# Start of a fused attention and feed-forward kernel: order of the w_in quarters, and of the first group's matmuls around the second chunk's numerators

## The chip, the cores and the metric

The kernel runs on one core of one Trainium2 chip. The core has a matrix engine (TensorE, PE in the profile), a vector engine (VectorE, DVE), an activation engine (ScalarE, ACT), a general engine (GpSimd, POOL) and SyncE (SP), which issues most DMA transfers. Each engine runs its own list of instructions in the written order and waits on semaphores for the others. The metric is the device time of one execution in microseconds; lower is better.

## The reference, cut to what matters

```python
# q, k, v: [4 batches, 4 heads, 1088 tokens, 32]; S1, S2: [8, 32]; w_in: [128, 2048]; w_out: [2048, 128]
def phi(x):                                # 64 features of a head's token
    a = einsum('rd,bhsd->bhsr', S1, x)
    b = einsum('rd,bhsd->bhsr', S2, x)
    return einsum('bhsi,bhsj->bhsij', a, b).reshape(..., 64)
q_p, k_p = phi(q), phi(k)
kv  = einsum('bhsf,bhsd->bhfd', k_p, v)    # sums over all tokens of a batch
z   = sum(k_p, axis=2)
num = einsum('bhsf,bhfd->bhsd', q_p, kv)
den = einsum('bhsf,bhf->bhs', q_p, z)[..., None] + 1e-06
x   = (num / den), heads side by side      # [4352 tokens, 128]
h   = x @ w_in
g   = h - tanh(h)
out = g @ w_out
```

All inputs and the output are 32-bit floats. The kernel uses `g @ w_out = x @ (w_in @ w_out) - tanh(h) @ w_out`, with bf16 operands in the feed-forward part.

## The kernel before

**Work.** A batch's 1088 tokens are 34 blocks of 32. The queries are handled in five chunks: chunk 0 is the first 12 blocks of batch 0, chunk 1 the other 22, and chunks 2 to 4 are batches 1 to 3. The feed-forward part runs over ten groups of tokens, of 12, 10, 12, 16, 16, 16, 16, 16, 14 and 8 blocks. Group 0 (384 tokens) is just chunk 0, group 1 (320 tokens) comes from chunk 1.

**Steps of a batch's keys** (names as in the lists of order). `kp` (PE, L553) projects the transposed keys `kT` (DVE, L542); `kab` (DVE, L559) transposes the result; `gram` (PE, L584), `gm` (DVE, L590) and `fold` (PE, L593) make the weights for the denominators; `wk` (DVE and POOL, L573) forms the key products; `sum` (PE, L609) adds them up against v. Then `kvz` (ACT, L619) copies the sums out of PSUM, `turn` (PE, L629) transposes them, and `ndw` (ACT, L636) copies the transposed sums to SBUF, as the weights of the numerators.

**Steps of a query chunk.** `qp` (PE, L679 for chunk 0, L700 for the others) projects, `qab` takes the result out of PSUM (ACT L691 for chunk 0, DVE L706), `au`, `dn`, `rd`, `an` make the denominators, `qm` (DVE and POOL, L724) the products, `qt` (DVE, L731) transposes them into `qpT`, `num` (PE, L746) multiplies them with `ndw` into PSUM banks 0 to 3, and `x` (L769; ACT for chunks 0 and 1) casts the result into the bf16 tile `xT`.

**Steps of a group.** There are 16 slices of 128 hidden units. For slice k, `h` (PE, L838) is the first layer, `t` (ACT, L841) the tanh of it, `o` (PE, L889) the second layer, added up in one bank. Slices are numbered through: group 0 has h0 to h15, group 1 h16 to h31, group 2 h32 and on. The h's rotate over three PSUM banks, so that h of slice k+3 has to wait until t of slice k has read its bank; o of slice k waits for t of slice k. For groups 7 to 9 the slices go in pairs (L829, L832), and the last group has a form of its own (L854).

**The weights.** w_in comes in four quarters of 512 columns (`wi0` to `wi3`, SP, L495), each cast to bf16 by `wic0` to `wic3` (L775, three on ACT and one on POOL). Slices 0 to 3 of each group need quarter 0, slices 4 to 7 quarter 1, and so on. Once all four are cast, SP issues a DMA transpose of w_in (`wT`, L782); from it PE computes w_in @ w_out (`wp`, L787), and DVE splits that product in two bf16 parts, `whi` and `wlo`. w_out comes in three pieces, cast by POOL (L778).

**The order.** Nothing is scheduled when the program is built. A table holds the list of steps of each engine, word for word; a second list (sessions) says in which order the users of each PSUM bank come; a third (gates) adds waits that only pace the loads and POOL's work (`k2.0<o9`: the load k2.0 waits for o9). Semaphore waits are worked out from the data, the banks and the gates. In PE's list, entries such as `$2` and `!1` are matmuls on constants whose result nobody reads.

Of the kernel before, what the change touches and what calls it, by code (L numbers as in the profile page):

```python
# [40 lines left out]
class Program:  # L41
# [203 lines left out]
DB = 7  # L245
QB = (1, 1)
QBASE = {1: 4}
WIC = ('scalar', 'gpsimd', 'scalar', 'scalar')
KCUTS = ((('vector', 0, 8), ('gpsimd', 22, 29), ('vector', 8, 16), ('gpsimd', 29, 36), ('vector', 16, 22)), (('gpsimd', 12, 24), ('vector', 0, 12), ('vector', 24, 30), ('gpsimd', 30, 36)), (('gpsimd', 12, 24), ('vector', 0, 12), ('vector', 24, 30), ('gpsimd', 30, 36)), (('gpsimd', 12, 24), ('vector', 0, 12), ('vector', 24, 30), ('gpsimd', 30, 36)))
SCUTS = (((0, 4), (4, 9)), ((0, 9),), ((0, 9),), ((0, 9),))  # L250
QCUTS = ((('vector', 0, 2), ('gpsimd', 2, 4)), (('gpsimd', 2, 4), ('vector', 0, 2)), (('gpsimd', 0, 2), ('gpsimd', 2, 4)), (('gpsimd', 0, 2), ('gpsimd', 2, 4)), (('gpsimd', 0, 2), ('gpsimd', 2, 4)))
# [20 lines left out]
ORDERS = {  # L272
    "tensor": """
~52 sk ~17 kp0 sk2 *4 ^1 gram0 qp0 fold0 *2 ^1 qpu0 sum0.0 sum0.4 qp1 turn0 $2 num0.0 num0.1 !1 h0 h1 h2 o0 h3 o1 h4
o2 h5 o3 h6 h7 kp1 h8 o4 h9 o5 h10 gram1 o6 h11 o7 fold1 h12 o8 h13 o9 num1.0 num1.1 h14 o10 h15 o11 o12 h30 h22 h20
wp h19 h18 h32 h31 o13 o14 h47 o15 h24 lin0.whi h16 lin0.wlo h17 qp2 h42 h23 lin1.whi h25 lin1.wlo o16 o17 h21 o18 o19
h29 o20 h28 h27 o21 o22 o23 h26 o24 o25 h34 h39 o26 o27 h38 o28 h43 kp2 h33 o29 o30 h35 o31 h46 h45 gram2 lin2.whi h40
fold2 lin2.wlo sum1.0 h36 h44 o32 o33 o34 turn1 o35 h37 h41 o36 num2.0 num2.1 o37 o38 o39 o40 o41 o42 h51 h49 o43 o44
# [25 lines left out]
x4.2 out6 out7 out8 out9.0  # L304
""",
    "gpsimd": """
id0 id1 au1.0 kTz0 qTz0 vz1 identb au1.1 kTz1 wqz vz0 wk0.22 wk0.29 qm0.2 qTz1 wic1 woc0 qm1.2 woc1 woc2 wk1.30 wk1.12
au2 an2 qm2.2 qm2.0 wk2.30 au3 wk2.12 an3 qm3.2 qm3.0 wk3.12 au4 wk3.30 an4 qm4.0 qm4.2
""",
    "sync": """  # L310
s2 k0.0 q0.1 q0.0 q0.2 v0.1 v0.0 v0.2 v0.3 wi0 wi3 wi2 wi1 wo0 k1.0 wo1 wo2 wT q1.0 k2.0 v1.0 q3.0 v1.1 st0.0.3
st0.0.1 v1.2 v1.3 v2.2 q2.0 st0.0.0 st0.0.2 v2.1 st2.0.2 st1.0.3 v3.1 v2.0 v2.3 v3.0 v3.3 st2.0.0 st1.0.1 st1.0.0
st2.0.1 st2.0.3 st1.0.2 k3.0 st3.0.0 st4.0.3 v3.2 st3.0.1 st3.0.2 st3.0.3 st4.0.0 st5.2.3 st5.0.3 st4.0.2 st4.0.1
st6.0.0 st6.0.2 st5.2.0 st5.0.2 st5.0.1 st5.2.1 st6.0.3 st5.0.0 st5.2.2 st7.0.0 st7.0.2 st7.0.3 st7.4.0 st7.4.2
# [24 lines left out]
def bass_polysketch_attn__then__act_tanh_shrink_kernel(nc, q, k, v, S1, S2, moe_w_in, moe_w_out, out):  # L339
# [20 lines left out]
    def act(n):  # L360
        return 75 + n / 1.2
# [411 lines left out]
    def casts():  # L773
        for x, eng in enumerate(WIC):
            P.op(f"wic{x}", eng, act(512) if eng == "scalar" else 620, lambda e, x=x, eng=eng: (e.copy if eng == "scalar" else e.tensor_copy)(  # L775
                w_in[:, 512 * x:512 * x + 512], w_in_f[:, 512 * x:512 * x + 512]), r=[("w_in_f", x)], w=[("w_in", x)])
# [216 lines left out]
```

## Time and profile before

| quantity | us |
|---|---|
| three runs | 104.47, 104.50, 105.26 |
| median of the runs | 104.5 |
| the profiled execution | 105.19 |
| its span, first to last instruction | 103.4 |
| PE busy | 94.6 (91%) |
| ACT busy | 78.6 (76%) |
| DVE busy | 54.4 (53%) |
| POOL busy | 34.8 (34%) |

The rows below and in the prediction are of the profiled execution, in microseconds from its first instruction; some 1.8 us of its time lie outside the span. The busy share of PE is high because matmuls are pipelined and overlap; what matters is where an engine stands still and for whom. The granted clock of PE was full in the whole span (the row of 40 slices):

```profile
PEclk9999999999999999999999999999999999999999
```

A row of the timeline has the start, the busy time, the engine, the line, the operation, the tiles written and read, the count of instructions that were merged, and in brackets the idle time just before with the engine that ended it. A row of the chain of waits has the start, the duration and the piece of work.

### The profile page before, as it was taken

The numbers are of one execution on the slowest core, as the hardware profiler recorded it, in microseconds if no ns is written. First come the engines' busy times: TensorE is split into PE (matmuls) and PEld (weight loads), VectorE is DVE, ScalarE is ACT, GpSimd is POOL, SyncE is SP. The second block draws the span as 40 slices with busy tenths as digits, with TensorE's granted clock in tenths as the row PEclk, the third lists the DMA queues.
The fourth block names the chain that finished last, engine by engine and source line by source line (L and its number), as shares of the span: only waits on it lengthen the run. The fifth ranks groups of instructions, "written<-read, shape, count | busy, mean of one in ns | idle before, by whom it ended". The sixth has DMA issues, their size and how long they took to land.

```text
span 103.4 us, 3175 instructions
## 1 busy us (share of the span) xinstructions
PE 94.6 (91%) x1358; PEld 49.3 (48%) x1370; DVE 54.4 (53%) x95; ACT 78.6 (76%) x156; POOL 34.8 (34%) x42
## 2 busy tenths in 40 slices
PE   7999778997999999999998999999999999999950
PEld 6647442455454665433544435345544434546740
DVE  2579997850975968884166936550756020020210
ACT  3212459858989862899996989889878999999930
POOL 2156469400655980028960000559910000000000
PEclk9999999999999999999999999999999999999999
DMA  2999999935078147037446100081031005404234
GB/s 70 360 243 271 368 319 172 301 85 202 6 222 205 40 141 182 0 63 193 86 74 205 37 6 0 1 150 27 10 53 23 6 0 79 73 6 76 39 60 95
DMA packets 25967, 11.76 MB, mean 114 GB/s; under 512 B 19808, under 2 KB 24416, under 8 KB 25952
## 3 DMA queue, kind: packets, MB, share of 16 engines
q1 hardware_dynamic: 25624, 11.15, 44.8%
q10 hardware_dynamic: 328, 0.40, 1.3%
q8 instruction: 11, 0.18, 0.7%
q14 instruction: 4, 0.03, 0.1%
HBM read 8.79 MB, written 2.23 MB: 107 GB/s over the span
## 4 chain that ended last, share of the span: by engine, by line
PE 70%; POOL 7%; DMA 6%; SPq 4%; ACT 3%; DVE 3%; issue 2%; POOLq 0%
PE ps L889 23%; PE ps L838 17%; PE ps L829 8%; PE ps L746 7%; DMA w_in_f<-in_moe_w_in_dram 6%; POOL qp L724 4%; PE ps L881 3%; PE ps L700 2%; PE ps L609 2%; PE ps L854 2%; PE ps L553 2%; ACT tt L841 2%; SPq L489 2%; POOL wk L573 1%; DVE qab L706 1%
## 5 line engine op out<-in xcount | busy, mean ns | idle before, releaser
L841 ACT ACTIVATE tt<-ps 128x512 bf16<-128x512 f32 (+2 forms) x112 | 52.7, 552 | 9.3 <-PE ps L838 5.0
L889 PE MATMUL ps<-tt,w_out 128*128 128x512 bf16 (+3 forms) x141 | 39.2, 355 | 0.5 <-ACT tt L841 0.3
L838 PE MATMUL ps<-xT,w_in 128*128 128x512 bf16 (+2 forms) x107 | 33.0, 353 | 2.4 <-ACT xT L769 1.3
L889 PEld LDWEIGHTS ps<-tt,w_out 128*128 128x128 bf16 x144 | 13.9, 98 | 12.6 <-issue 1.1
L832 ACT ACTIVATE tt<-ps 128x1024 bf16<-128x1024 f32 (+2 forms) x24 | 18.4, 859 | 0.5
L838 PEld LDWEIGHTS ps<-xT,w_in 128*128 128x128 bf16 x112 | 10.0, 98 | 17.4 <-ACT tt L841 10.8
L724 POOL TENSOR_TENSOR qp<-an,qab 128x1152 f32<-128x1152 f32 (+2 forms) x8 | 15.4, 1925 | 2.9 <-DVE an L717 2.4
L731 DVE STREAM_TRANSPOSE qpT<-qp 128x1152 f32<-128x1152 f32 (+2 forms) x10 | 11.2, 1126 | 8.7 <-POOL qp L724 8.7
L573 POOL TENSOR_TENSOR wk<-kab 128x384 f32<-128x384 f32 (+2 forms) x8 | 9.0, 1126 | 20.0 <-PE ps L889 19.5
L894 DVE STREAM_TRANSPOSE osb<-ps 128x512 f32<-128x512 f32 (+3 forms) x9 | 5.9, 657 | 17.4 <-PE ps L889 17.0
L829 PE MATMUL ps<-xT,w_in 128*128 128x512 bf16 (+2 forms) x48 | 12.1, 335 | 0.1
L746 PE MATMUL ps<-qpT,ndw 32*32 32x288 f32 (+4 forms) x320 | 6.9, 352 | 0.4 <-DVE qpT L731 0.3
L829 PEld LDWEIGHTS ps<-xT,w_in 128*128 128x128 bf16 x48 | 4.5, 98 | 4.6 <-ACT tt L832 1.2
L542 DVE STREAM_TRANSPOSE kT<-kraw 128x512 f32<-128x512 f32 (+1 forms) x8 | 5.6, 720 | 1.0 <-DMA kraw<-in_k_dram 1.0
L706 DVE STREAM_TRANSPOSE qab<-ps 128x1152 f32<-128x1152 f32 (+1 forms) x4 | 5.1, 1273 | 1.4 <-PE ps L700 1.4
L769 DVE CAST xT<-ps 128x576 bf16<-128x576 f32 (+2 forms) x7 | 4.4, 686 | 2.7 <-PE ps L746 2.7
L711 POOL TENSOR_TENSOR au<-qab 128x288 f32<-128x288 f32 x3 | 2.4, 791 | 10.0 <-DVE qab L706 7.0
L656 DVE STREAM_TRANSPOSE qT<-qraw 128x1088 f32<-128x1088 f32 (+2 forms) x5 | 5.3, 1065 | 0.7 <-DMA qraw<-in_q_dram 0.7
L746 PEld LDWEIGHTS ps<-qpT,ndw 32*32 32x32 f32 x320 | 4.0, 103 | 3.2 <-DVE qpT L731 2.0
L559 DVE STREAM_TRANSPOSE kab<-ps 128x576 f32<-128x576 f32 x4 | 3.1, 773 | 3.6 <-PE ps L553 3.6
L424 PE MATMUL ps<-const-bfloat16-1.0 128*32 128x256 bf16 x69 | 4.2, 417 | 0.8 <-PEq L978 0.8
L609 PE MATMUL ps<-wk,vx 128*32 128x64 f32 x288 | 4.8, 220 | 0.0
(82 smaller groups left out, 78.8 us busy)
## 6 DMA issues: line engine op xcount, KB each, us to landing
kraw<-in_k_dram SPq DMA_DIRECT2D x3, 544.0 KB, 4.9
qraw<-in_q_dram SPq DMA_DIRECT2D x3, 544.0 KB, 3.8
vx<-in_v_dram SPq DMA_DIRECT2D x8, 144.0 KB, 3.0
vx<-in_v_dram SPq DMA_DIRECT2D x8, 128.0 KB, 3.2
w_in_f<-in_moe_w_in_dram SPq DMA_DIRECT2D x4, 256.0 KB, 6.1
out_dram<-osb SPq DMA_DIRECT2D x12, 64.0 KB, 2.0
out_dram<-osb SPq DMA_DIRECT2D x12, 48.0 KB, 2.2
w_out_f<-in_moe_w_out_dram SPq DMA_DIRECT2D x2, 256.0 KB, 7.5
```

Source lines behind the costliest of these rows:

```text
L573: P.op(f"wk{b}.{n0}", eng, (dve if eng == "vector" else pool)(64 * n), lambda e, n0=n0, n1=n1, n=n, a_=a_: e.tensor_tensor(out=wk[0][:, n0 ...
L609: ins = e.matmul(ps[32 * h:32 * h + 32, SB, 0:64], vx[i][:, h, t, :], wk[0][:, 4 * t + h, :], start=(t == 0), stop=(t == 8), tile_position ...
L706: P.op(f"qab{u}", "vector", dve(32 * n), lambda e: e.transpose(out=qab[ui][:, 0:n, :].rearrange("p (h t) x -> p h t x", h=H), in_=ps[:, b0 ...
L724: P.op(f"qm{u}.{h0}", eng, (pool if eng == "gpsimd" else dve)(64 * (n1 - n0)), lambda e, n0=n0, n1=n1, b_=b_: e.tensor_tensor(out=qp[ui][: ...
L731: P.op(f"qt{u}.{h0}", "vector", dve(64 * (n1 - n0)), lambda e, n0=n0, n1=n1: e.transpose(out=qpT[ui][:, n0:n1, :, :].rearrange("p n y j -> ...
L746: ins = e.matmul(ps[32 * h:32 * h + 32, ct, 0:32 * own[ct]], ndw[i][32 * ct:32 * ct + 32, y, 32 * h:32 * h + 32], qpT[ui][32 * ct:32 * ct ...
L829: P.op(f"h{s + y}", "tensor", pe(n), lambda e, jb=jb, b0=b0, y=y: e.matmul(ps[:, b0 + y, 0:n], w_in[:, 128 * (jb + y):128 * (jb + y) + 128 ...
L832: P.op(f"t{s}", "scalar", act(2 * n), lambda e, ts=ts, b0=b0: e.activation(out=tt[:, ts:ts + 2, 0:n], in_=ps[:, b0:b0 + 2, 0:n], func=AF.T ...
L838: P.op(f"h{s}", "tensor", pe(n), lambda e, jb=jb, bk=bk: e.matmul(ps[:, bk, 0:n], w_in[:, 128 * jb:128 * jb + 128], xT[:, t0:t0 + n], star ...
L841: P.op(f"t{s}", "scalar", act(n), lambda e, ts=ts, bk=bk: e.activation(out=tt[:, ts, 0:n], in_=ps[:, bk, 0:n], func=AF.Tanh, scale=-1.0), ...
L889: P.op(f"o{slot + jb}", "tensor", pe(n), lambda e, jb=jb, ts=ts: e.matmul(acc[:, 0:n], w_out[:, jb, :], tt[:, ts, 0:n], start=late and jb ...
L894: P.op(f"out{g}", "vector", dve(n), lambda e: e.transpose(out=osb[u][:, 0:n], in_=acc[:, 0:n]), r=ka, w=[("osb", u)], prio=when)
```

## The change

Four things are moved; no instruction is added or removed.

- The quarters of w_in are loaded in the order 0, 1, 2, 3 (before: 0, 3, 2, 1).
- The quarter that POOL casts is the last of w_in (before: quarter 1). It keeps its place in POOL's list, and it is the transfer issued fourth in both kernels.
- On ACT, the sums' copies `kvz0` and `ndw0` stand right behind the first cast; the other two casts follow them.
- On PE, in group 0, `kp1` moves from behind h7 to behind o3, ahead of h6. h6 to h9 then follow without o's between, `gram1` has one o less ahead of it, `fold1` one o less and one h (h12) more, and `num1` (the numerators of chunk 1) goes from between o9 and h14 to behind h15. The list of bank users follows.

```diff
-WIC = ('scalar', 'gpsimd', 'scalar', 'scalar')
+WIC = ('scalar', 'scalar', 'scalar', 'gpsimd')
...
     "tensor": """
...
-o2 h5 o3 h6 h7 kp1 h8 o4 h9 o5 h10 gram1 o6 h11 o7 fold1 h12 o8 h13 o9 num1.0 num1.1 h14 o10 h15 o11 o12 h30 h22 h20
+o2 h5 o3 kp1 h6 h7 h8 h9 o4 h10 gram1 o5 h11 o6 h12 fold1 o7 h13 o8 h14 o9 h15 num1.0 num1.1 o10 o11 o12 h30 h22 h20
...
     "scalar": """
-k0.1 s1 act0 kap0 wq0u qab0 wic0 wic3 kvz0 ndw0 wic2 x0.0 t0 t1 t2 t3 t4 t5 t6 t7 t8 t9 t10 t11 t12 t13 t14 t15 x1.0
+k0.1 s1 act0 kap0 wq0u qab0 wic0 kvz0 ndw0 wic1 wic2 x0.0 t0 t1 t2 t3 t4 t5 t6 t7 t8 t9 t10 t11 t12 t13 t14 t15 x1.0
...
     "gpsimd": """
-id0 id1 au1.0 kTz0 qTz0 vz1 identb au1.1 kTz1 wqz vz0 wk0.22 wk0.29 qm0.2 qTz1 wic1 woc0 qm1.2 woc1 woc2 wk1.30 wk1.12
+id0 id1 au1.0 kTz0 qTz0 vz1 identb au1.1 kTz1 wqz vz0 wk0.22 wk0.29 qm0.2 qTz1 wic3 woc0 qm1.2 woc1 woc2 wk1.30 wk1.12
...
     "sync": """
-s2 k0.0 q0.1 q0.0 q0.2 v0.1 v0.0 v0.2 v0.3 wi0 wi3 wi2 wi1 wo0 k1.0 wo1 wo2 wT q1.0 k2.0 v1.0 q3.0 v1.1 st0.0.3
+s2 k0.0 q0.1 q0.0 q0.2 v0.1 v0.0 v0.2 v0.3 wi0 wi1 wi2 wi3 wo0 k1.0 wo1 wo2 wT q1.0 k2.0 v1.0 q3.0 v1.1 st0.0.3
```

The instructions of ACT at the start, before. The cast behind `d_wi0` is that of the first quarter; `d_wi3` is the semaphore of the quarter that is loaded second:

```order
L691 COPY qab<-ps 128x12x16
L775 CAST w_in<-w_in_f 128x512 [waits d_wi0]
L775 CAST w_in<-w_in_f 128x512 [waits d_wi3]
L619 COPY kvz<-ps 128x256 [waits s_tensor]
L636 COPY ndw<-ps 128x256 [waits s_tensor]
L775 CAST w_in<-w_in_f 128x512 [waits d_wi2]
L769 CAST xT<-ps 128x384 [waits s_tensor]
```

The same place of ACT's list after:

```order
L691 COPY qab<-ps 128x12x16
L775 CAST w_in<-w_in_f 128x512 [waits d_wi0]
L619 COPY kvz<-ps 128x256 [waits s_tensor]
L636 COPY ndw<-ps 128x256 [waits s_tensor]
L775 CAST w_in<-w_in_f 128x512 [waits d_wi1]
L775 CAST w_in<-w_in_f 128x512 [waits d_wi2]
L769 CAST xT<-ps 128x384 [waits s_tensor]
```

The copy of the sums and the copy of their transpose no longer stand behind a cast that waits for the second transfer; two casts now stand between them and the cast of chunk 0's numerators.

PE in group 0, before, from o2 (the first row) to gram1; each L838 row is one h or more, each L889 row an o, L553 is kp1 and L584 gram1:

```order
L889 MATMUL ps<-tt,w_out 128x384
L838 MATMUL ps<-xT,w_in 128x384
L889 MATMUL ps<-tt,w_out 128x384
L838 MATMUL ps<-xT,w_in 128x384 x2
L553 MATMUL ps<-kT1,wkm 32x288 x8
L838 MATMUL ps<-xT,w_in 128x384
L889 MATMUL ps<-tt,w_out 128x384
L838 MATMUL ps<-xT,w_in 128x384
L889 MATMUL ps<-tt,w_out 128x384
L838 MATMUL ps<-xT,w_in 128x384
L584 MATMUL ps<-kab1 32x32 x9
```

The same stretch after, from o2 to gram1:

```order
L889 MATMUL ps<-tt,w_out 128x384
L838 MATMUL ps<-xT,w_in 128x384
L889 MATMUL ps<-tt,w_out 128x384
L553 MATMUL ps<-kT1,wkm 32x288 x8
L838 MATMUL ps<-xT,w_in 128x384 x4
L889 MATMUL ps<-tt,w_out 128x384
L838 MATMUL ps<-xT,w_in 128x384
L584 MATMUL ps<-kab1 32x32 x9
```

kp1 stands two h's earlier; h6 to h9 come behind it in one piece, and one o (o5) less stands ahead of gram1.

And PE at the end of group 0, after, from fold1 (L593) to the first rows of num1 (L746); before, the L746 rows stood right behind the second L889 row that follows fold1, with two h's still to come:

```order
L593 MATMUL ps<-gm,s2f 128x32
L889 MATMUL ps<-tt,w_out 128x384
L838 MATMUL ps<-xT,w_in 128x384
L889 MATMUL ps<-tt,w_out 128x384
L838 MATMUL ps<-xT,w_in 128x384
L889 MATMUL ps<-tt,w_out 128x384
L838 MATMUL ps<-xT,w_in 128x384
L746 MATMUL ps<-qpT1,ndw0 32x192 x2
L746 MATMUL ps<-qpT1,ndw0 32x160 x2
```

All of group 0's h's are now ahead of num1, and o10 to o12 behind it.

More of the change, by code (lines that the diff above doesn't have):

```diff
@@ L320 @@
 SESSIONS = """
-sk sk2 kp0 kap0 gram0 qp0 sum0 qp1 num0 h0 h1 h2 lin0 h3 h4 h5 h6 h7 kp1 h8 h9 h10 gram1 h11 h12 h13 num1 h14 h15 h30
+sk sk2 kp0 kap0 gram0 qp0 sum0 qp1 num0 h0 h1 h2 lin0 h3 h4 h5 kp1 h6 h7 h8 h9 h10 gram1 h11 h12 h13 h14 h15 num1 h30
 h22 h20 wp h19 h18 h32 h31 h47 h24 h16 h17 qp2 h42 h23 lin1 h25 h21 h29 h28 h27 h26 h34 h39 h38 h43 kp2 h33 h35 h46
```

## The prediction

> **What bounds the kernel now.** I read the chain of waits in order of time first. It says which work the end hangs on. Its start, as far as the change reaches:
>
> ```profile
> 5.42 6.00 DMA w_in_f<-in_moe_w_in_dram
> ...
> 11.44 0.62 ACT w_in L775
> ...
> 12.38 0.44 PE ps L629 x2
> ...
> 13.37 1.00 PE ps L746 x58
> ```
>
> The second w_in transfer lands at 5.42 + 6.00 = 11.42 us; only when its cast is through do the sums' copy kvz0, the turn, the numerators num0, their cast x0.0 and the first h follow. Then ACT's timeline, for what stands around those casts and for group 0's tanhs:
>
> ```profile
> 9.98 0.62 ACT L775 CAST w_in<-w_in_f 128x512 bf16<-128x512 f32 x1 [0.68 <-DMA w_in_f<-in_moe_w_in_dram]
> ...
> 11.96 0.36 ACT L619 COPY kvz<-ps 128x256 f32<-128x256 f32 x1
> 12.85 0.37 ACT L636 COPY ndw<-ps 128x256 f32<-128x256 f32 x1 [0.53 <-PE ps L629]
> 13.12 0.62 ACT L775 CAST w_in<-w_in_f 128x512 bf16<-128x512 f32 x1
> 14.39 0.48 ACT L769 CAST xT<-ps 128x384 bf16<-128x384 f32 x1 [0.65 <-PE ps L746]
> 15.30 3.18 ACT L841 ACTIVATE tt<-ps 128x384 bf16<-128x384 f32 x8 [0.43 <-PE ps L838]
> 18.67 1.26 ACT L841 ACTIVATE tt<-ps 128x384 bf16<-128x384 f32 x3 [0.19 <-PE ps L838]
> 20.15 0.49 ACT L841 ACTIVATE tt<-ps 128x384 bf16<-128x384 f32 x1 [0.23 <-PE ps L838]
> ...
> 22.79 0.87 ACT L841 ACTIVATE tt<-ps 128x384 bf16<-128x384 f32 x2 [1.06 <-PE ps L838]
> 23.55 0.82 ACT L769 CAST xT<-ps 128x384 bf16<-128x384 f32 x2
> ```
>
> ACT starts a tanh every 0.39 us (0.87 for two that last 0.48 to 0.49 each, overlapped), so 16 of them would need 6.3 us; from 15.30 to 23.66 they take 8.36. The largest hole, 1.06, is before t14: PE runs num1 before h14. And x1.0, which group 1 waits for, stands behind t15. PE's timeline shows the rest of group 0, with kp1 (L553), gram1 (L584), fold1 (L593) and num1 (L746):
>
> ```profile
> 9.83 1.21 PE L609 MATMUL ps<-wk,vx 128*32 128x64 f32 x72
> 10.97 0.90 PE L700 MATMUL ps<-qT,wq 32*32 32x192 f32 x32
> ...
> 17.00 0.34 PE L889 MATMUL ps<-tt,w_out 128*128 128x384 bf16 x1
> 17.18 0.54 PE L838 MATMUL ps<-xT,w_in 128*128 128x384 bf16 x2
> 17.65 0.72 PE L553 MATMUL ps<-kT,wkm 64*32 64x288 f32 x16
> 18.30 0.34 PE L838 MATMUL ps<-xT,w_in 128*128 128x384 bf16 x1
> ...
> 19.31 0.38 PE L584 MATMUL ps<-kab 128*32 128x32 f32 x18
> 19.62 0.34 PE L889 MATMUL ps<-tt,w_out 128*128 128x384 bf16 x1
> ...
> 20.25 0.41 PE L593 MATMUL ps<-gm,s2f 128*128 128x32 f32 x2
> 20.49 0.33 PE L838 MATMUL ps<-xT,w_in 128*128 128x384 bf16 x1
> ...
> 20.98 0.33 PE L889 MATMUL ps<-tt,w_out 128*128 128x384 bf16 x1
> 21.23 1.25 PE L746 MATMUL ps<-qpT,ndw 32*32 32x192 f32 x64
> ```
>
> Behind num1 and the o's around it nothing is reordered.
>
> **Part one: the sums' copies ahead of the casts.** The sums end at 9.83 + 1.21 = 11.04, and kvz0 could have run at 11.1; it ran at 11.96, behind the cast of the second quarter. With the new order kvz0 runs 11.1 to 11.47. PE is then still in chunk 1's projection (10.97 + 0.90 = 11.87), which stands ahead of the turn in its list and becomes the next bound: the next matmul can start 0.07 before such a modelled end (18.30 against 17.65 + 0.72), so the turn starts at 11.80 and not at 12.38. From there every step keeps its distance: ndw0 0.47 behind the turn (12.27), num0 0.52 behind ndw0 (12.79), x0.0 1.02 behind num0. Gain of the part: **0.58 us**, x0.0 at 13.81. The transposed products that num0 also waits for must be there by then:
>
> ```profile
> 11.69 1.04 DVE L731 STREAM_TRANSPOSE qpT<-qp 128x384 f32<-128x384 f32 x2
> ...
> 15.11 1.37 DVE L542 STREAM_TRANSPOSE kT<-kraw 128x512 f32<-128x512 f32 x2
> ...
> 18.47 0.78 DVE L559 STREAM_TRANSPOSE kab<-ps 128x576 f32<-128x576 f32 x1 [0.94 <-PE ps L553]
> ...
> 20.11 0.96 DVE L731 STREAM_TRANSPOSE qpT<-qp 128x768 f32<-128x768 f32 x1
> ```
>
> The first row ends at 12.73, in front of 12.79; DVE's list is the same, and nothing up to kT1 waits for ACT's moved steps.
>
> The two casts now behind ndw0 hide in the wait for num0. They start 0.27 behind ndw0's start (as 13.12 did behind 12.85), at 12.54, and 0.52 apart (as 11.44 and 11.96 stand), so the second runs 13.06 to 13.68, 0.13 before x0.0. That cover is thin. x0.0 stands behind the casts in ACT's list, and a late quarter holds it. The new second quarter is the transfer that landed at 11.42. The third lands between that and the fourth:
>
> ```profile
> 12.87 0.61 POOL L775 CAST w_in<-w_in_f 128x512 bf16<-128x512 f32 x1 [0.66 <-DMA w_in_f<-in_moe_w_in_dram]
> ```
>
> The fourth landed just before 12.87, so no quarter can hold either cast by much: if the second only came with the fourth, the casts would start at 12.87 and 13.39, and x0.0 at 13.91, 0.10 later than in the sum. That prices the risk of a landing out of order. The Trainium skill (DMA: Bandwidth & Descriptors, Queues, rings and completion order) does say that completion is not in order of issue within one issuing engine. By that rule the gain of this part could be 0.48 instead of 0.58; the rows of this trace, 9.98, 11.44 and 12.87 for the first, second and fourth, agree with landing in order, and I take that.
>
> The load order itself and POOL's cast cost nothing: all quarters are of one size, POOL's cast waits for the fourth transfer before and after, and is through at 13.48 in both; h12 needs it some 5 us later. The transpose of w_in needs all four casts, and the last is through at 13.68 here, 13.74 before.
>
> ```profile
> 7.32 0.51 SPq L466 DMA_DIRECT2D kraw<-in_k_dram  x1
> ...
> 13.77 3.59 SPq L782 DMA_TRANSPOSE w_inT<-w_in  x1
> ```
>
> So the loads behind it in SP's list (q1.0 with its wait for t0 first) are not held longer.
>
> **Part two: group 0 in its new order.** Group 0 now starts with t0 at 15.30 - 0.58 = 14.72. In the trace o3 starts at 17.00, when t3 began at 15.30 + 3 x 0.39 = 16.47, so PE sees a tanh done 0.53 after its start; and a tanh starts 0.37 after its h (18.30, 18.67). Hence o3 at 16.42. kp1 comes 0.27 behind the matmul ahead of it (17.65 behind h7 at 17.38, the second of the 17.18 pair): 16.69. kp1 also needs kT1, ready at 15.11 + 1.37 = 16.48: covered, by 0.2. h6 follows 0.65 behind kp1 (18.30 - 17.65), at 17.34, and t6 at 17.71. Without kp1 it would have been 14.72 + 6 x 0.39 = 17.06: the move **costs** ACT 0.65 here, where before it cost 0.19 at t8 and, by gram1's wait for kab1, 0.23 at t11.
>
> Then t7 at 18.10, h10 at 18.63 when PE sees t7 done, gram1 at 18.90. gram1 no longer waits: kab1 starts 0.82 behind kp1 (18.47 - 17.65), so at 17.51, and is done at 18.29. From gram1 on PE sets the pace: o5 0.31 behind it (19.62 - 19.31), then 0.16 a matmul (three of them from 20.49 to 20.98): h11 19.37, o6 19.53, h12 19.69, fold1 0.24 later at 19.93, o7 another 0.24 later (20.49 - 20.25) at 20.17, and o9, the fifth matmul from o7 on, and h15 at 20.82 and 20.98. Each h's bank is free by then (h15's tanh t12 starts at 20.13, seen at 20.66). num1 stands 0.25 behind the last matmul (21.23 - 20.98): at **21.23**, just where it was. Its transposed products are earlier than before: by the durations 0.78 and twice 0.96, with gm1 between, DVE ends qt1.0 at about 20.4, while it ended at 21.07.
>
> num1 takes 1.25, and x1.0 follows 0.02 later as x0.0 did (13.37 + 1.00 to 14.39): x1.0 at 22.50 against 23.55. t15 (h15 at 20.98) is through at 21.9, so ACT waits 0.6 for num1. It is num1 that is late next, no longer the tanhs. Group 1's first h needs x1.0 and moves with it. **Sum of both parts: 1.05 us**, of which 0.58 is part one's.
>
> **Behind group 1.** What could not move with it is what hangs on absolute times. The rows that could hold it:
>
> ```profile
> 24.51 1.06 PE L787 MATMUL ps<-w_out,w_inT 128*128 128x128 bf16 x16
> ...
> 26.79 2.44 POOL L573 TENSOR_TENSOR wk<-kab 128x384 f32<-128x384 f32 x2 [7.61 <-PE ps L889]
> ...
> 41.79 10.25 ACT L841 ACTIVATE tt<-ps 128x512 bf16<-128x512 f32 x20 [2.35 <-PE ps L746]
> ...
> 80.24 18.85 ACT L832 ACTIVATE tt<-ps 128x1024 bf16<-128x1024 f32 x24
> ```
>
> The view of the transposed w_in's tile adds how long its transfer took to land:
>
> ```profile
> DMA to landing us min/median/max: 5.7/5.7/5.7
> ```
>
> That is 13.77 + 5.7 = 19.5, before wp at 24.51 - 1.0 = 23.5. POOL's long wait is released by an o, chunk 2's projections stand in PE's list, and the loads' gates are steps of PE and ACT: all move along. At 41.79 ACT waits for num2, whose inputs hang on those steps; at the end ACT runs 18.85 us without a gap. I take the whole 1.05.
>
> **The sum.** 105.19 - 1.05 = 104.14 for the profiled execution. That one is 0.7 above the median of the runs, 104.5; taken from the median the changed kernel runs in 103.45, say **103.5 us**. No change means within 1%, about what a measurement of this kernel can tell: 103.45 to 105.55. The forecast lies on that edge.
>
> **Rivals.**
> *Larger gain.* If kp1 holds PE less, or num1 starts earlier, ACT's tanhs are the bound: x1.0 cannot be before t15's end at 21.9, and the gain is at most 23.55 - 21.9 = 1.6, 102.9. For it: num1's products are ready at 20.4. Against: num1 stands behind h15 in PE's list.
>
> *Smaller gain by the landing.* The 0.58 hangs on the second quarter landing at 11.42 in this slow execution. In the 104.5 runs it may have landed 0.7 earlier; then kvz0 was not held there and only 1.05 - 0.58 = 0.47 is left: 104.0. For it: the transfer heads the chain. Against: any other transfer can make 0.7.
>
> *Nothing is left at the end.* If num2's chain held to absolute times, ACT's 2.35 us before 41.79 would just grow: 104.5. Against: each step of it is released by PE or ACT.
>
> *Slower.* The load of k1 sets kp1's new place, which has 0.2 of cover against 17.65 - 16.48 = 1.17 before.
>
> ```profile
> DMA to landing us min/median/max: 2.9/3.5/7.8
> ```
>
> By this row of the k loads its landing was at most 7.32 + 7.8 = 15.12, and kT1 begins at 15.11: this transfer already sets that. Each microsecond that it lands later now holds h6, and with it everything. From 1.05 + 0.2 = 1.25 us later (16.4) the gain is gone; at another 1.05 later, 2.3 in all, the kernel is 1% slower, 105.55. Against: the k1 load keeps its place behind the quarters.
>
> **Chances.** Forecast with 0.7 to 1.3 us of gain, 103.2 to 103.8: 0.55. Larger gain: 0.12. Smaller by the landing: 0.15. Nothing left: 0.10. Slower: 0.08. About half of the forecast's share lies beyond the edge of 1%; with the larger gain and its near cases that makes 0.42 faster, 0.50 within 1%, 0.08 slower. The range from the larger gain to no gain, 102.9 to 104.5, leaves out some 2 in 10 at its ends.
>
> **What would show it.** In the changed profile: kvz0 at 11.1 and the turn at 11.8 with no cast ahead; x0.0 near 13.8; kp1 near 16.7 and a hole of some 0.6 us in ACT between t5 and t6; gram1 without a wait near 18.9; num1 at 21.2 and x1.0 near 22.5 with ACT waiting for it; and the wait before the first 512-wide tanh, 41.79 before, near 40.8. A later kp1 or a shift that shrinks behind 23 us would show it wrong.

## The result and the profile after

The changed kernel takes 104.3 us (median of 20 runs, 103.66 to 105.65) against 105.25 us for the kernel before, run on the same chip (median of 20, 104.47 to 106.69). The ratio is 0.9916 with a 95% interval of 0.9887 to 0.9945: 0.84% faster, some 0.9 us. Measured once more later (`e11_changed_again`), the changed kernel gave 0.9889 (0.9848 to 0.9930). The three runs that the prediction went by (median 104.5) lay low: the profiled execution of before, 105.19, was a usual one. Executions more than 1.5% above the fastest of their kernel are left out of the ratios; the profile of `e9_early_block` below is of one of these, and only its holes are read from it.

The profiled execution after took 104.69 us, its span is 101.8 (before 105.19 and 103.4). So 2.9 us of its time lie outside the span, against 1.8 before: the gain of this one pair is 0.5 in the time and 1.6 in the span, and neither is the gain of the change. ACT's timeline of the changed kernel, from the sums' copy to x1.0:

```profile
11.37 0.37 ACT L619 COPY kvz<-ps 128x256 f32<-128x256 f32 x1 [0.40 <-PE ps L609]
12.27 0.37 ACT L636 COPY ndw<-ps 128x256 f32<-128x256 f32 x1 [0.53 <-PE ps L629]
12.54 1.14 ACT L775 CAST w_in<-w_in_f 128x512 bf16<-128x512 f32 x2
13.81 0.48 ACT L769 CAST xT<-ps 128x384 bf16<-128x384 f32 x1
14.71 2.41 ACT L841 ACTIVATE tt<-ps 128x384 bf16<-128x384 f32 x6 [0.43 <-PE ps L838]
17.99 4.08 ACT L841 ACTIVATE tt<-ps 128x384 bf16<-128x384 f32 x10 [0.86 <-PE ps L838]
22.68 0.81 ACT L769 CAST xT<-ps 128x384 bf16<-128x384 f32 x2 [0.61 <-PE ps L746]
```

kvz0 waits for the sums and no longer for a cast; the two casts are one row of 1.14 that ends at 13.68, before x0.0; x0.0 is at 13.81 (14.39 before). The one hole in group 0's tanhs is now before t6, 0.86 long, and x1.0 waits 0.61 for num1. x1.0 is at 22.68 where it was at 23.55: **0.87 us gained**.

PE's timeline of the changed kernel: chunk 1's projection, the turn, kp1, gram1 and num1:

```profile
11.23 0.62 PE L700 MATMUL ps<-qT,wq 32*32 32x192 f32 x32
11.79 0.44 PE L629 MATMUL ps<-ident,kvz 128*128 128x128 f32 x2
...
16.96 0.72 PE L553 MATMUL ps<-kT,wkm 64*32 64x288 f32 x16 [0.21 <-DVE kT L542]
...
19.18 0.38 PE L584 MATMUL ps<-kab 128*32 128x32 f32 x18
...
21.36 1.25 PE L746 MATMUL ps<-qpT,ndw 32*32 32x192 f32 x64
```

kp1 waits for kT1, which the prediction had covered by 0.2. The start of the chain of waits of the changed kernel (start, duration, piece) shows who took over:

```profile
2.06 4.20 DMA qraw<-in_q_dram
6.35 0.58 DVE qT L656
...
13.89 0.60 DVE au L711
15.63 1.29 DVE kT L542 x2
```

Before, the chain began with the second quarter of w_in; no transfer of w_in is in it now. It runs from the first q load through DVE's list to kT1 and kp1, then to t6.

Behind x1.0 everything moved by the same amount. The two later tanh rows of the prediction, and the copy of the last output, on ACT after:

```profile
40.92 10.25 ACT L841 ACTIVATE tt<-ps 128x512 bf16<-128x512 f32 x20 [2.36 <-PE ps L746]
...
79.34 18.84 ACT L832 ACTIVATE tt<-ps 128x1024 bf16<-128x1024 f32 x24
98.70 0.27 ACT L868 COPY osr<-ps 128x128 f32<-128x128 f32 x1 [0.52 <-PE ps L854]
99.05 0.63 ACTq L871 DMA_DIRECT2D out_dram<-osr  x1
```

The same end on ACT before:

```profile
99.61 0.27 ACT L868 COPY osr<-ps 128x128 f32<-128x128 f32 x1 [0.52 <-PE ps L854]
99.97 0.64 ACTq L871 DMA_DIRECT2D out_dram<-osr  x1
```

The shift is 0.87 at 40.92, 0.90 at 79.34, 0.91 at the last copy. The span is shorter by 1.6; the other 0.7 is the landing of the last store, from the end of its issue to the end of the span 2.1 us after (101.8 - 99.68) and 2.8 before (103.4 - 100.61). Nothing in the change touches that store, and the times of the runs differ by 0.9, not by 1.6.

### The profile page after: what moved, and what is told of

It reads as the page before. It is cut to its first block, busy times and chain, and to the rows that moved or that the text cites. A ratio compares the mean times of both kernels' runs of the same rounds, so it can differ in the third digit from the quotient of the medians.

```text
span 101.8 us, 3175 instructions
## 1 busy us (share of the span) xinstructions
PE 93.5 (92%) x1358; PEld 48.7 (48%) x1370; DVE 54.8 (54%) x95; ACT 78.5 (77%) x156; POOL 34.7 (34%) x42
## 4 chain that ended last, share of the span: by engine, by line
PE 68%; DVE 13%; POOL 7%; DMA 4%; issue 2%; SPq 1%; ACT 1%; DVEq 0%; POOLq 0%
PE ps L889 23%; PE ps L838 16%; PE ps L829 8%; PE ps L746 6%; POOL qp L724 4%; DMA qraw<-in_q_dram 4%; PE ps L881 3%; DVE qpT L731 2%; PE ps L700 2%; PE ps L609 2%; DVE qab L706 2%; PE ps L553 2%; PE ps L854 2%; DVE wk L573 2%; POOL wk L573 1%
## 5 line engine op out<-in xcount | busy, mean ns | idle before, releaser
L889 PE MATMUL ps<-tt,w_out 128*128 128x512 bf16 (+3 forms) x141 | 39.0, 355 | 0.5 <-ACT tt L841 0.3
L838 PE MATMUL ps<-xT,w_in 128*128 128x512 bf16 (+2 forms) x107 | 32.7, 353 | 2.0 <-ACT tt L841 0.7
L889 PEld LDWEIGHTS ps<-tt,w_out 128*128 128x128 bf16 x144 | 13.9, 98 | 12.8 <-issue 1.4
L838 PEld LDWEIGHTS ps<-xT,w_in 128*128 128x128 bf16 x112 | 9.9, 97 | 16.9 <-ACT tt L841 11.0
L746 PE MATMUL ps<-qpT,ndw 32*32 32x288 f32 (+4 forms) x320 | 6.9, 352 | 0.4 <-DVE qpT L731 0.3
L746 PEld LDWEIGHTS ps<-qpT,ndw 32*32 32x32 f32 x320 | 4.0, 103 | 3.2 <-DVE qpT L731 2.0
L609 PEld LDWEIGHTS ps<-wk,vx 128*32 128x32 f32 x288 | 4.2, 110 | 0.7 <-issue 0.7
```

The lines of the kernel that those rows point to most:

```text
L609: ins = e.matmul(ps[32 * h:32 * h + 32, SB, 0:64], vx[i][:, h, t, :], wk[0][:, 4 * t + h, :], start=(t == 0), stop=(t == 8), tile_position ...
L746: ins = e.matmul(ps[32 * h:32 * h + 32, ct, 0:32 * own[ct]], ndw[i][32 * ct:32 * ct + 32, y, 32 * h:32 * h + 32], qpT[ui][32 * ct:32 * ct ...
L838: P.op(f"h{s}", "tensor", pe(n), lambda e, jb=jb, bk=bk: e.matmul(ps[:, bk, 0:n], w_in[:, 128 * jb:128 * jb + 128], xT[:, t0:t0 + n], star ...
L889: P.op(f"o{slot + jb}", "tensor", pe(n), lambda e, jb=jb, ts=ts: e.matmul(acc[:, 0:n], w_out[:, jb, :], tt[:, ts, 0:n], start=late and jb ...
```

## The experiments

The yardstick in all of them is the stretch from x0.0 to x1.0 on ACT, which holds part two (and, where kT1 is late, kp1's wait for it), and the start of x0.0, which holds part one.

**Each part alone.** `e1_copies_only` is the kernel before with the loads, the casts and the copies of the change, and PE's old order:

```diff
-WIC = ('scalar', 'gpsimd', 'scalar', 'scalar')
+WIC = ('scalar', 'scalar', 'scalar', 'gpsimd')
...
-k0.1 s1 act0 kap0 wq0u qab0 wic0 wic3 kvz0 ndw0 wic2 x0.0 t0 t1 t2 t3 t4 t5 t6 t7 t8 t9 t10 t11 t12 t13 t14 t15 x1.0
+k0.1 s1 act0 kap0 wq0u qab0 wic0 kvz0 ndw0 wic1 wic2 x0.0 t0 t1 t2 t3 t4 t5 t6 t7 t8 t9 t10 t11 t12 t13 t14 t15 x1.0
```

> Part one alone: the loads, the casts and ACT's order of the changed kernel, PE's order of the kernel before. Theory (the two parts have separate causes): the turn near 11.8, x0.0 near 13.8, and all of group 0 moves up by 0.58 us, since kp1 at 17.07 is still behind the end of kT1 (16.5 to 16.9); x1.0 at 22.97 against 23.55 before and 22.68 changed, the first 512-wide tanh at 41.2 against 41.79 and 40.92, time 0.55% below before. Rival (VectorE's list sets when num1's products are ready, so an earlier start of group 0 is lost again at num1): x0.0 at 13.8 but x1.0 at 23.4 to 23.6, no gain.

`e2_pe_order_only` is the kernel before with PE's new order alone:

```diff
-o2 h5 o3 h6 h7 kp1 h8 o4 h9 o5 h10 gram1 o6 h11 o7 fold1 h12 o8 h13 o9 num1.0 num1.1 h14 o10 h15 o11 o12 h30 h22 h20
+o2 h5 o3 kp1 h6 h7 h8 h9 o4 h10 gram1 o5 h11 o6 h12 fold1 o7 h13 o8 h14 o9 h15 num1.0 num1.1 o10 o11 o12 h30 h22 h20
```

> Part two alone: PE's order of the changed kernel, loads, casts and ACT's order of the kernel before. Theory (separate causes): x0.0 at 14.39 as before, kp1 at 17.27 with no wait for kT1, h6 at 17.92, a hole of 0.65 us in ACT before t6, num1 at 21.81, x1.0 at 23.08, the first 512-wide tanh at 41.3, time 0.45% below before. Rival (the reorder of group 0 pays only with the earlier start, or not at all): x1.0 at 23.5 or later, no gain.

Measured: 0.9936 (0.9894 to 0.9978) and 0.9931 (0.9892 to 0.9969). ACT's timeline of `e1_copies_only`, with the old hole before t14:

```profile
13.92 0.48 ACT L769 CAST xT<-ps 128x384 bf16<-128x384 f32 x1
...
22.31 0.87 ACT L841 ACTIVATE tt<-ps 128x384 bf16<-128x384 f32 x2 [1.06 <-PE ps L838]
23.07 0.82 ACT L769 CAST xT<-ps 128x384 bf16<-128x384 f32 x2
```

ACT's timeline of `e2_pe_order_only`:

```profile
11.89 0.36 ACT L619 COPY kvz<-ps 128x256 f32<-128x256 f32 x1
...
14.32 0.48 ACT L769 CAST xT<-ps 128x384 bf16<-128x384 f32 x1 [0.65 <-PE ps L746]
...
18.21 4.08 ACT L841 ACTIVATE tt<-ps 128x384 bf16<-128x384 f32 x10 [0.58 <-PE ps L838]
22.90 0.81 ACT L769 CAST xT<-ps 128x384 bf16<-128x384 f32 x2 [0.61 <-PE ps L746]
```

Each part pays alone. x0.0 is 0.47 earlier in the first (14.39 - 13.92) where 0.58 was forecast, and from x0.0 to x1.0 it is 8.58 in the second against 9.16 before, 0.58 less where 0.47 was forecast. With the copies where they were, kvz0 again runs at 11.89 behind the second cast. The sum, 1.05, is the forecast one, but only because the two misses of 0.11 cancel; the profile of the changed kernel shows 0.87, since there x0.0 to x1.0 is 8.87 (13.81 to 22.68). The difference is in the hole before t6, 0.58 in `e2_pe_order_only` and 0.86 there: group 0 starts half a microsecond later in `e2_pe_order_only`, and kp1 does not wait for kT1.

**The two moves of part two.** `e3_kp1_back` is the changed kernel with kp1, gram1 and fold1 at their old places and num1 behind h15; `e4_num1_back` keeps kp1 early and puts num1 back. The row of `e3_kp1_back`:

```diff
-o2 h5 o3 kp1 h6 h7 h8 h9 o4 h10 gram1 o5 h11 o6 h12 fold1 o7 h13 o8 h14 o9 h15 num1.0 num1.1 o10 o11 o12 h30 h22 h20
+o2 h5 o3 h6 h7 kp1 h8 o4 h9 o5 h10 gram1 o6 h11 o7 fold1 h12 o8 h13 o9 h14 h15 num1.0 num1.1 o10 o11 o12 h30 h22 h20
```

> The changed kernel with kp1, gram1 and fold1 back at their old places in PE's list; num1 stays behind h15. Theory (kp1's early place costs, num1's late place pays): kp1 at 17.07, no hole before t6, holes of about 0.3 us before t8, t11 and t12, num1 at 21.06, x1.0 at 22.33 against 22.68 in the changed kernel, the first 512-wide tanh at 40.6, 0.3% faster than the changed kernel. Rival (the early kp1 is what pays, by an earlier kab1 and no wait of gram1): x1.0 at 22.97 or later, slower than the changed kernel.

The row of `e4_num1_back` against the changed kernel's:

```diff
-o2 h5 o3 kp1 h6 h7 h8 h9 o4 h10 gram1 o5 h11 o6 h12 fold1 o7 h13 o8 h14 o9 h15 num1.0 num1.1 o10 o11 o12 h30 h22 h20
+o2 h5 o3 kp1 h6 h7 h8 h9 o4 h10 gram1 o5 h11 o6 h12 fold1 o7 h13 o8 o9 num1.0 num1.1 h14 o10 h15 o11 o12 h30 h22 h20
```

> The changed kernel with num1 back at its old place behind o9 and ahead of h14, o10 and h15; kp1 stays early. Theory (kp1's early place costs, num1's late place pays): kp1 near 16.96, num1 at 21.05, a hole of about 1 us in ACT before t14, x1.0 at 23.36, the first 512-wide tanh at 41.6, within 0.3% of before although group 0 starts 0.58 us earlier. Rival (the early kp1 is what pays): x1.0 at 22.7 or earlier, as fast as the changed kernel.

Measured: 0.9887 (0.9850 to 0.9924) for `e3_kp1_back` and 0.9952 (0.9919 to 0.9984) for `e4_num1_back`. ACT's timeline of `e4_num1_back`:

```profile
14.05 0.48 ACT L769 CAST xT<-ps 128x384 bf16<-128x384 f32 x1
...
17.94 3.32 ACT L841 ACTIVATE tt<-ps 128x384 bf16<-128x384 f32 x8 [0.58 <-PE ps L838]
22.54 0.87 ACT L841 ACTIVATE tt<-ps 128x384 bf16<-128x384 f32 x2 [1.28 <-PE ps L838]
23.30 0.82 ACT L769 CAST xT<-ps 128x384 bf16<-128x384 f32 x2
```

kp1 early without num1 late leaves both holes, 0.58 and 1.28, and 9.25 us from x0.0 to x1.0: 0.09 more than before. ACT's timeline of `e3_kp1_back`, with num1 late and kp1 at its old place:

```profile
13.94 0.48 ACT L769 CAST xT<-ps 128x384 bf16<-128x384 f32 x1
...
22.53 0.81 ACT L769 CAST xT<-ps 128x384 bf16<-128x384 f32 x2 [0.49 <-PE ps L746]
```

The stretch is 8.59 (13.94 to 22.53), the whole gain. So part two's gain is num1's place, and kp1's move is worth nothing.

**A third order.** In `e6_kp1_back_num1_early` kp1 stays behind h7, and num1 stands behind h15 with one o fewer (o9) ahead of it; o5 and o6 stand ahead of gram1, so that only two o's are left between gram1 and num1:

```diff
-o2 h5 o3 kp1 h6 h7 h8 h9 o4 h10 gram1 o5 h11 o6 h12 fold1 o7 h13 o8 h14 o9 h15 num1.0 num1.1 o10 o11 o12 h30 h22 h20
+o2 h5 o3 h6 h7 kp1 h8 o4 h9 o5 h10 o6 h11 gram1 o7 h12 fold1 h13 o8 h14 h15 num1.0 num1.1 o9 o10 o11 o12 h30 h22 h20
```

> The changed kernel with PE's group 0 in a third order: kp1 behind h7, the h's as early as their banks allow, o6 ahead of h11 and gram1, o9 to o12 behind num1. Theory (num1's place, and the work in front of it, is what is late next in the changed kernel): kp1 at 17.1, num1 near 20.8, x1.0 near 22.1 against 22.68 in the changed kernel and 22.53 with kp1 back alone, the first 512-wide tanh near 40.4, 1.3% below before. Rival (PE's whole work up to group 1 is the bound, so that the o's put off come back behind num1): x1.0 earlier, but the first 512-wide tanh at 40.9 as in the changed kernel.

Measured: 0.9862 (0.9814 to 0.9911); from x0.0 to x1.0 8.20 (14.10 to 22.30), 0.39 less than the changed kernel's order where kT1 holds nothing (8.59, `e11_changed_again` below). It was run again beside the changed kernel on one chip:

> The changed kernel once more, beside the third order on the same chip. Theory: 0.8% to 1.0% below before, x1.0 between 22.4 and 22.8, the hole in ACT before t6 0.58 us (kp1 not held by kT1) or somewhat more (held).

> The third order of group 0 once more (kp1 behind h7, o6 ahead of gram1, num1 behind h15, o9 to o12 put off), beside the changed kernel on the same chip. Theory (kp1's early place costs, and the o's ahead of num1 hold it): 0.4 us below the changed kernel, 1.2% to 1.4% below before, x1.0 near 22.2. Rival (the difference seen so far is that of the chips and of the transfers' landings): the same as the changed kernel within 0.2%.

Measured: the changed kernel 0.9889 (0.9848 to 0.9930), the third order 0.9869 (0.9827 to 0.9912). ACT's timeline of `e11_changed_again`:

```profile
13.98 0.48 ACT L769 CAST xT<-ps 128x384 bf16<-128x384 f32 x1
...
17.88 4.08 ACT L841 ACTIVATE tt<-ps 128x384 bf16<-128x384 f32 x10 [0.58 <-PE ps L838]
22.57 0.81 ACT L769 CAST xT<-ps 128x384 bf16<-128x384 f32 x2 [0.61 <-PE ps L746]
```

ACT's timeline of `e12_third_order_again`:

```profile
11.89 0.62 ACT L775 CAST w_in<-w_in_f 128x512 bf16<-128x512 f32 x1 [2.44 <-DMA w_in_f<-in_moe_w_in_dram]
12.42 0.37 ACT L619 COPY kvz<-ps 128x256 f32<-128x256 f32 x1
...
14.85 0.48 ACT L769 CAST xT<-ps 128x384 bf16<-128x384 f32 x1
...
23.01 0.81 ACT L769 CAST xT<-ps 128x384 bf16<-128x384 f32 x2 [0.45 <-PE ps L746]
```

The stretch is 8.16 here and 8.59 in the changed kernel, as expected of the order. But the first quarter of w_in came only at 11.89, held kvz0 until 12.42, and the profile's x1.0 is later than the changed kernel's. In the times the two kernels differ by 0.2% with intervals that overlap: the third order beats the kernel before twice; that it beats the changed kernel is not shown.

In `e11_changed_again`, the changed kernel, kp1 does not wait for kT1, the hole before t6 is 0.58, and the stretch is 8.59 instead of 8.87.

**The loads.** `e8_old_load_order` is the changed kernel with the load order and POOL's quarter of before:

```diff
-WIC = ('scalar', 'scalar', 'scalar', 'gpsimd')
+WIC = ('scalar', 'gpsimd', 'scalar', 'scalar')
...
-k0.1 s1 act0 kap0 wq0u qab0 wic0 kvz0 ndw0 wic1 wic2 x0.0 t0 t1 t2 t3 t4 t5 t6 t7 t8 t9 t10 t11 t12 t13 t14 t15 x1.0
+k0.1 s1 act0 kap0 wq0u qab0 wic0 kvz0 ndw0 wic3 wic2 x0.0 t0 t1 t2 t3 t4 t5 t6 t7 t8 t9 t10 t11 t12 t13 t14 t15 x1.0
```

> The changed kernel with the old load order 0, 3, 2, 1 and quarter 1 cast by GpSimd; the sums' copies stay ahead of the casts. Theory (load order and the engine of the last cast are worth nothing by themselves): x0.0, kp1 and x1.0 as in the changed kernel, 13.8 to 14.05, 16.7 to 17.0 and 22.5 to 22.9. Rival (they matter): h4, which now needs the quarter that lands fourth, is late, and t4 waits.

It was run once, in 103.24 us: x0.0 at 13.64 and x1.0 at 22.23, each some 0.2 earlier than expected, and the stretch 8.59, that of the changed kernel. No tanh waits for a quarter. So this execution shows no gain from the new order of the loads and from the other engine for the last cast; more than one execution can't show.

**What held the turn.** In most profiles PE stands still inside chunk 1's projection (L700) for no wait that the profile shows. The projection's weight loads (PEld) in `e3_kp1_back`; the turn follows at 11.93:

```profile
10.64 0.15 PEld L700 LDWEIGHTS ps<-qT,wq 32*32 32x32 f32 x9
11.41 0.21 PEld L700 LDWEIGHTS ps<-qT,wq 32*32 32x32 f32 x23 [0.62 <-issue]
```

Seven of the ten profiles with this start of PE's list have the hole, 0.17 to 0.70 long in these rows. It is always behind the eighth matmul and the ninth weight load, and it ends between 11.1 and 11.8. The other three, in which the projection only begins at 10.91 to 11.41 (the changed kernel's at 11.23), have none. The theory was that a block of PE's instructions arrives there and that the fixed place can be moved. `e5_half_dummies` replaces 69 constant matmuls of 256 columns at the start by 35 of 512, 68 instructions fewer (a matmul and its weight load each):

```diff
-~52 sk ~17 kp0 sk2 *4 ^1 gram0 qp0 fold0 *2 ^1 qpu0 sum0.0 sum0.4 qp1 turn0 $2 num0.0 num0.1 !1 h0 h1 h2 o0 h3 o1 h4
+~26 sk ~9 kp0 sk2 *4 ^1 gram0 qp0 fold0 *2 ^1 qpu0 sum0.0 sum0.4 qp1 turn0 $2 num0.0 num0.1 !1 h0 h1 h2 o0 h3 o1 h4
...
-        one = nc.const_aps.tensor(1.0, [128, 256], BF16)
+        one = nc.const_aps.tensor(1.0, [128, 512], BF16)
```

> The changed kernel with 69 short constant matmuls of 256 columns at PE's start turned into 35 of 512 columns: the same PE time with 68 instructions fewer ahead of chunk 1's projection qp1. In the runs so far PE stood still inside qp1, always behind its 8th matmul, until 11.2 to 11.5 us, with no engine to wait for (0.17 us in the kernel before, 0.50 to 0.70 in four other kernels). Theory (PE stands at a fixed place of its instruction stream and waits for the next block of instructions, an instruction transfer that arrives at about 11.3): the place moves 68 instructions on, into num0; qp1 runs in one piece of 0.6 us, the turn at 11.3 instead of 11.8 to 12.0, x0.0 near 13.4 instead of 13.8 to 14.05; kp1 is then held by kT1 at 16.6 to 16.7, and x1.0 comes near 22.4 against 22.68. Rival (qp1 waits for data or a PSUM bank): the hole stays behind qp1's 8th matmul until 11.2 to 11.5, the turn near 11.9, x0.0 near 13.9, x1.0 as in the changed kernel.

Measured: 1.0045 (1.0000 to 1.0089); the median of all its executions is 106.41. PE's timeline of `e5_half_dummies`:

```profile
10.85 0.62 PE L700 MATMUL ps<-qT,wq 32*32 32x192 f32 x32
11.41 0.44 PE L629 MATMUL ps<-ident,kvz 128*128 128x128 f32 x2
...
12.40 0.36 PE L746 MATMUL ps<-qpT,ndw 32*32 32x96 f32 x6
14.28 0.94 PE L746 MATMUL ps<-qpT,ndw 32*32 32x96 f32 x58 [1.52 <-issue]
```

The place is as the theory has it: the projection runs in one piece, the turn is 0.4 earlier, and the hole now lies 68 instructions on, in num0. Its end is not: the hole ends at 14.28 instead of 11.1 to 11.8. At 1.52 it costs more than it gave. `e7_both`, the third order with the same constant matmuls, came out alike:

> The third order of group 0 together with the longer, fewer constant matmuls at PE's start. Theory (instruction block, then kT1): turn at 11.3, x0.0 near 13.4, kp1 at 16.7 held by kT1, num1 near 20.3, x1.0 near 21.6, the first 512-wide tanh near 39.9, 1.8% below before. Rival (waits for data in qp1): as the third order alone, x1.0 near 22.1.

Measured: 1.0003 (0.9970 to 1.0036), median of all its executions 105.57; the hole is 1.57 at the same matmul. Two kernels were then to have the block asked for earlier, by 22 instructions more ahead of gram0:

```diff
-~52 sk ~17 kp0 sk2 *4 ^1 gram0 qp0 fold0 *2 ^1 qpu0 sum0.0 sum0.4 qp1 turn0 $2 num0.0 num0.1 !1 h0 h1 h2 o0 h3 o1 h4
+~52 sk ~17 kp0 sk2 ~16 gram0 qp0 fold0 *2 ^1 qpu0 sum0.0 sum0.4 qp1 turn0 $2 num0.0 num0.1 !1 h0 h1 h2 o0 h3 o1 h4
```

> The changed kernel with the four constant matmuls of 512 columns and the one of 256 ahead of gram0 turned into 16 short ones of 256: the same PE time, 22 instructions more, all of them behind kp0. With 68 instructions fewer the hole of PE moved exactly 68 instructions on, into num0, and the packet of the instruction queue started between 11 and 12 us instead of between 8.5 and 9. Theory (a block of instructions is asked for when PE comes to a fixed place some 256 instructions ahead of the block's end, and takes about 3 to 4 us): that place moves up from gram0 (7.3) to the end of kp0 (about 5.5), the block is there by 9.5, the packet starts at 5.5 to 7, and no hole is left in front of or in qp1; turn at 11.3, x0.0 near 13.3, kp1 held by kT1 at 16.6 to 16.7, x1.0 near 22.4, 1.1% below before. The next hole could come 128 matmuls on, near kp1 at 16 us. Rival (the block comes when the loads leave room, at 11.3 whatever asks for it): the hole stands at the end of the sums, kvz0 comes only near 11.8 and x0.0 near 14, no better than the changed kernel.

> The third order of group 0 (kp1 behind h7, num1 behind h15 with o9 to o12 put off) together with the 16 short constant matmuls ahead of gram0. Theory: no hole in qp1, x0.0 near 13.3, kp1 near 16.7 held by kT1, num1 near 20.4, x1.0 near 21.7 against 22.30 with the third order alone, the first 512-wide tanh near 40.0, 1.9% below before. Rival (the block comes at 11.3 whatever asks for it): as the third order alone or up to 0.4 us later, x1.0 at 22.3 to 22.7.

Measured: 0.9956 (0.9916 to 0.9995) on the changed kernel and 0.9939 (0.9902 to 0.9977) on the third order, by the middle values less gain than without, with intervals that overlap. PE's timeline of `e9_early_block`:

```profile
9.83 1.20 PE L609 MATMUL ps<-wk,vx 128*32 128x64 f32 x69
11.86 0.30 PE L609 MATMUL ps<-wk,vx 128*32 128x64 f32 x3 [0.83 <-issue]
...
17.52 0.70 PE L553 MATMUL ps<-kT,wkm 64*32 64x288 f32 x13
18.60 0.67 PE L553 MATMUL ps<-kT,wkm 64*32 64x288 f32 x3 [0.37 <-issue]
```

The hole came 22 instructions earlier, now in the sums, which kvz0 waits for, and ended no sooner (11.86, and 11.19 in `e10_third_order_early_block`); a second one appeared in kp1. That the holes sit at a fixed count of instructions is shown by the moves, 68 on and 22 back. That it is a block of instructions in transfer rests on the times of a queue, "q8 instruction" in the profile, which moves 10 packets in 0.16 MB, so 16 KB each. In all eleven profiles with a hole, its first packet ends 1.3 to 1.6 us ahead of the hole's end: at 9.70 for 11.29 in the kernel before, at 10.10 for 11.41 in `e3_kp1_back`, at 12.91 for 14.28 in `e5_half_dummies`, at 10.38 for 11.86 in `e9_early_block`. The second packet of `e9_early_block` ends at 16.92, 1.7 ahead of the end of the hole in kp1. In the changed kernel's profile it ended at 9.67, and the projection came too late to wait for it. So the hole follows the packet; that PE waits for just this packet the profile does not say. What sets the packet's start stays open: with 68 instructions fewer it started at 11.80 and 11.68, elsewhere at 7.7 to 9.4, and with 22 more at 9.14 and 8.60, where 5.5 to 7 was expected.

## Why the prediction was right, and where its sizes were off

- **Part one, right.** The turn was forecast at 11.80, ndw0 at 12.27, num0 at 12.79 and x0.0 at 13.81; they came at 11.79, 12.27, 12.79 and 13.81. The casts hid, no cast waited for a later quarter, and load order and POOL's cast showed no cost (`e8_old_load_order`). The exact hit is partly luck. The sums ended 0.26 later than before, at 11.30, and the projection had no hole; in the trace of before it had one, whose end set the 11.87 that the term stood on. `e1_copies_only` gave 0.47 of the 0.58. Over the six profiles that have the copies ahead, PE's start as it was, and kvz0 not held by the first cast, x0.0 stands at 13.64 to 14.05; in the two with the copies at their old place it stands at 14.39 and 14.32.
- **The step that was mis-sized: "kp1 also needs kT1, ready at 15.11 + 1.37 = 16.48: covered, by 0.2."** kT1 ended at 16.90 and held kp1 until 16.96 instead of 16.69. DVE's timeline of the changed kernel has the reason:

```profile
6.35 0.58 DVE L656 STREAM_TRANSPOSE qT<-qraw 128x384 f32<-128x384 f32 x1 [1.09 <-DMA qraw<-in_q_dram]
...
13.89 0.59 DVE L711 TENSOR_TENSOR au<-qab 128x192 f32<-128x192 f32 x1
...
15.54 1.36 DVE L542 STREAM_TRANSPOSE kT<-kraw 128x512 f32<-128x512 f32 x2
```

  The first two in DVE's timeline of before:

```profile
6.09 0.58 DVE L656 STREAM_TRANSPOSE qT<-qraw 128x384 f32<-128x384 f32 x1 [0.66 <-DMA qraw<-in_q_dram]
...
13.63 0.36 DVE L711 TENSOR_TENSOR au<-qab 128x192 f32<-128x192 f32 x1
```

  A q load 0.26 later and an `au` 0.23 longer moved kT1 from 15.11 to 15.54, by more than the cover. The `au` took 0.36 to 0.76 over the profiles. Here POOL's cast of w_out (L778) had begun at 13.66, ahead of it; before, the cast began behind it, at 13.70, and was the longer one itself, 0.76 against 0.61. That the two hinder each other fits these times and was not tested apart. In `e11_changed_again`, where kT1 began at 15.20, the group started 0.17 later and the cover held, and kp1 came 2.88 behind x0.0, just the forecast distance (16.69 - 13.81). So the step is right in some executions and not in others: a cover of 0.2 is within what one load or one operation varies by.
- **Part two, right in its mechanism.** The hole before t6, gram1 without a wait, ACT waiting 0.6 for num1 (0.61): all there. The forecast put t6 0.65 later than six steps of 0.39 from t0. By that count it was 0.65 in `e11_changed_again` and 0.94 with the wait for kT1; the idle times in the rows, 0.58 and 0.86, are shorter because two tanhs overlap a little. num1 was forecast at 21.23 and came at 21.36; x1.0 at 22.50 and came at 22.68. That num1 is only 0.13 late after a kp1 0.27 late is luck: fold1 and the step behind it took 0.30 (20.15 - 19.99 and 20.29 - 20.15) where the sum had 0.48. And x1.0 came 0.07 behind num1's end, where the sum had 0.02. Without the wait for kT1 the stretch from x0.0 is 8.59, the forecast one 8.69. What the prediction did not see is that kp1's move, with its cost of 0.65, gains nothing over the old place (`e3_kp1_back`).
- **Behind group 1, right.** The shift is rigid in this pair of profiles, 0.87 to 0.91 from x1.0 to the last copy; nothing here hung on absolute times.
- **The sum.** 1.05 us was forecast, 0.87 to 0.91 is in the profile, and the ratios of the two measurements make 0.9 and 1.2 us. **The step that moved the absolute time was "taken from the median the changed kernel runs in 103.45".** From 105.19, which is next to the median 105.25 of 20, the sum gave 104.14, next to the measured median of 104.3; the base of three runs was 0.7 too low. The profiled execution itself took 104.69, since more of its time lay outside the span.
- **The rivals.** *Larger gain*: not seen with this order; num1 is late because of what PE has ahead of it, as said against it, and the third order frees 0.4 of it. *Smaller by the landing* assumed that the profiled execution of before lay above the usual ones: it did not, and part one alone is worth 0.64% (0.22 to 1.06) over the runs of `e1_copies_only`. *Nothing left*: fell with the rigid shift. *Slower*: its resource is real, though not in this pair. In both profiles kT1 started with no wait for a load, behind DVE's own list. kT1 waited for the k1 load in most of the other profiles, by 0.21 to 0.54, with kT1's start at 15.0 to 16.2; a landing late enough to cost more than tenths was not met.

## What to carry to other kernels

When a copy that others wait for stands behind a cast that waits for a transfer, move the copy ahead and check that the cast still hides; here the first cast of numerators came 0.3 to 0.75 us earlier for it, by single profiles. A hole on the engine that sets the pace can be closed by moving the long matmuls behind the short ones that feed it, and each move is worth testing alone, since one of two may do all the work. A cover of a few tenths of a microsecond over a transfer is no cover, and the base of a forecast should be a time whose place among the runs is known.

## What was not expected of the hardware

- **Holes at a fixed count of instructions.** PE stood still for 0.2 to 0.7 us with no wait that the profile shows, at the same instruction in seven of ten profiles; 68 instructions fewer ahead moved the hole by 68, and it grew to 1.5 us. The Trainium skill (Runtime: NRT & Kernel Launch, Instruction fetch mechanics) says that instructions stream in 16 KiB blocks of 256 and that crossing into the next is mostly hidden. The 1.52 us above do not agree, if such a block is what they wait for.
- **The clock fell after such a hole, in most executions.** A window of `e7_both` (the stretch, its length, busy time and count of PE, PEld, DVE, ACT and POOL, then the granted TensorE clock, the DMA share and GB/s):

```profile
16.00:18.50 2.50, 2.47 (x8) 0.94 (x9) 1.79 (x3) 1.75 (x4) 2.24 (x3) 0.51 1.32 152
```

  The same window of `e5_half_dummies`:

```profile
16.00:18.50 2.50, 2.15 (x26) 0.72 (x24) 1.50 (x2) 2.33 (x6) 2.24 (x3) 1.00 1.29 162
```

  After a hole of 1.57 us the clock was 0.51 from 16 to 18.5; with one of 1.52 at the same matmul it stayed at 1.00. Over all 22 executions of the two kernels the mean granted clock of the span was 0.979 to 0.984 in 14 and 0.993 or more in 8. In the 110 executions of the kernel before and the changed kernel that have a clock on record, it was never under 0.993. So the drop goes with the long hole in num0; why it comes in two of three executions is not shown. Of the 24 executions with the hole in the sums, one had 0.952, the others 0.988 or more.
- **The first quarter of w_in varies by some 2.4 us.** Its cast began at 9.44 (`e2_pe_order_only`) to 11.89 (`e12_third_order_again`), and since it still stands ahead of kvz0 it held kvz0 in two profiles (`e6_kp1_back_num1_early` and `e12_third_order_again`). A kernel with the first cast behind kvz0 as well was not tried.
- **The last store's landing** took 2.1 us in one profile and 2.8 in the other, for the same transfer: nearly as much as the change is worth.
